# Weight sums stored through GpSimd's queue, the size pass over w2 in halves to another buffer, and spread requests that wait on evacuations, in a two-layer attention and SwiGLU kernel

## Chip, cores and metric

The kernel runs on one core of one Trainium2 chip. The metric is the device time of one execution in microseconds (us), and the number for a kernel is the median of several executions. Profiled executions give in addition a span, which is the time from the first to the last recorded instruction.

## What is computed

The input x is 2048 tokens by 1024 channels in bf16. Two layers, each with the same weights, are applied: attention block A, feed-forward block B, then A and B again, each on a normalised x and with a residual.

```
def A(x):                              # 32 heads of 32 channels
    q, k, v = split(x @ wqkv)          # wqkv: 1024 x 3072
    # each token sees itself and 7 earlier ones, at distances 0, 2, 4, ... 14
    logits = einsum(q, k[idx]) * 32 ** -0.5, masked where idx < 0
    return (softmax(logits) @ v[idx]) @ wo        # wo: 1024 x 1024

def B(x):
    return (silu(x @ w1) * (x @ w3)) @ w2         # w1, w3: 1024 x 3584, w2: 3584 x 1024

x = x + A(layernorm(x)); x = x + B(layernorm(x))
x = x + A(layernorm(x)); x = x + B(layernorm(x))
```

## The kernel before

**Units.** The tokens are cut into four chunks of 512. A unit is one chunk in the B block of one layer, so there are eight units, numbered 0 to 7. The order is skewed: while B works on one chunk, the attention of the next one is computed by VectorE (DVE), and from unit 1 on a q, k, v projection for layer 1 follows a unit. TensorE (PE) does the projections (line 740, `ps`), the output projection of attention (line 688, `po`), w1 (line 1097, `pg`), w3 (line 1106, `pu`), w2 (line 1128, `acc`), and two kinds of small matmuls for attention: `gather` (line 513, tile L) collects the logits of the heads, and `spread` (line 554, tile pe) spreads the softmax weights over the channels again. ScalarE (ACT) does the silus and the copies out of PSUM. PSUM has six banks in the pool `psum`, which all large products share, and two in the pool `side`, for po, L, pe and the sizes.

**Two ways through B.** Units 0 and 1 multiply with the plain weights. Beside that they prepare the weights for the other six units: those use a scheme with seven products of half size in place of eight, on sums and differences of quarters of the weights in fp16. The scaled quarters and their sums are stored to DRAM, in `t_d` for w1 (made in unit 0) and w3 (made in unit 1), and in `t2_d` for w2 (made in unit 1). Units 2 to 7 load them as tiles early, late and t (lines 639 and 630) and multiply in lines 985 and 920.

**How a group is prepared.** The 28 blocks of 128 hidden channels are split as 16 and 12 (`fsplits`), and a group holds four blocks, so each of w1 and w3 has seven groups. `measure` (line 766) sums the squares of a group on ACT. `scales` makes a power of two from it (line 780 on PE, lines 771 to 775 on DVE). `copies` (line 792) writes four scaled quarters with ACT into one of two blocks of the buffer `big`, once for a = 0 and once for a = 1. `differences` (line 804) makes four differences from them with DVE and then stores the block, in lines 806 and 807, as 512 and 384 KB. The next `copies` into the same block must wait until those two transfers have read it. `prepare` places these steps at slots 0 to 7 of a group, which are the places after each pg and each pu. The second differences of a group come in slot 1 of the next one.

**w2.** Unit 0 measures w2: `measure2` (line 831) squares a tile of eight or six blocks of 512 and writes the squares, which nobody reads, into the start of `big`. In unit 1 `transform2` makes the sums: for each f it writes four scaled quarters with ACT (line 848) into block f % 2 of `big`, and its inner function `rest`, called one step later, makes four differences on DVE (line 854) and stores 896 KB in one transfer (line 856). There are eight such steps in the first split and six in the second, one for each group of `acc` products. The q, k, v projection that follows unit 1 evacuates its products into other parts of `big` (line 744), which overlap these blocks.

**Order.** Each engine runs its instructions in the order in which the Python code emits them, apart from POOL (GpSimd), on which no work stands after the start. The code keeps a model of time, `now`, with one clock for PE, DVE, ACT, SP and the DMA, and the functions `pe`, `dve`, `act` and `dma` advance it. `background(until)` emits as much of DVE's queued work (norms, sums, values, scores) as the model expects to fit before a given time; so a changed cost or due time changes the order on all engines from there on. Requests for the small attention matmuls stand in `pe_queue`, first in first out; `pe_requests` emits the head of it once the model's time of PE is 1.5 past the head's due time. `score_steps` appends one request for gather and four for spread in each half chunk; each spread is followed by a copy on ACT (line 556) into At, which frees its bank. All loads and stores go through SP's queue. Weight tiles share six buffers (`wp`), and a load is emitted when a buffer is released. `hsum` is a buffer of sums of activations, which only units 2 to 7 use.

Of the kernel before, what the change touches and what calls it, by code (L numbers as in the profile page):

```python
# [7 lines left out]
FP32 = mybir.dt.float32  # L8
BF16 = mybir.dt.bfloat16
# [3 lines left out]
ACTF = mybir.ActivationFunctionType  # L13
# [4 lines left out]
def kernel(  # L18
# [13 lines left out]
    nc = tc.nc  # L32
    cfg = dict(cfg or {})
    P = 128
# [33 lines left out]
    const = ctx.enter_context(tc.tile_pool(name="const", bufs=1))  # L68
# [28 lines left out]
    def dve(cost, ready=0.0):  # L97
        now["dve"] = max(now["dve"], ready) + cost
        return now["dve"]

    def act(cost, ready=0.0, table=None):
        t = max(now["act"], ready)
        if table is not None and table != now["table"]:
            now["table"] = table
            t += TABLE
        now["act"] = t + cost
        return now["act"] + 0.1
# [91 lines left out]
    size = const.tile([P, 2, NG], FP32, name="size")  # L199
    up_scale = const.tile([P, 2, NG], FP32, name="up_scale")  # L200
    down_scale = const.tile([P, 2, NG], FP32, name="down_scale")
    size2 = const.tile([P, 8], FP32, name="size2")
    total = const.tile([P, 1], FP32, name="total")
    down2 = const.tile([P, 1], FP32, name="down2")
    up2 = const.tile([P, 1], FP32, name="up2")
# [265 lines left out]
        vT = qkvp.tile([P, KT, HALO + TCH], BF16, name="vT")  # L471
        vs[l, h] = vT, load_part(vT, l, 2, h * TCH, True)

    pe_queue = []
    L_at, At_at, Ats, av_done = {}, {}, {}, set()
    halves = [(l, h) for l in range(2) for h in range(NCH * R)]
    BLK = TCH // 4

    def pe_requests(limit=1, must=False):

        while pe_queue and limit and (must or pe_queue[0][0] + 1.5 <= now["pe"]):
            pe_queue.pop(0)[1]()
            limit -= 1

    def score_steps():

        V = nc.vector
        for g, (l, h) in enumerate(halves):
            load_qk(l, h)
            while (l, h) not in qks:  # L490
                yield "blocked"
                load_qk(l, h)
            load_v(l, h)
            qT, kT, ready = qks[l, h]
            psm = wk.tile([P, W, TCH], BF16, name="psm")

            def mul_qk(w_):
                pr = scr.tile([P, KT, TCH], BF16, name="pr", tag="scr")
                k0 = HALO - DIL * w_
                V.tensor_tensor(pr[:], qT[:], kT[:, :, k0:k0 + TCH], op=ALU.mult)  # L500
                return pr

            yield 0.0, ready, lambda: None
            yield from tree(W, mul_qk, lambda w_: psm[:, w_, :])
            load_v(l, h)
            if g + 1 < len(halves):
                load_qk(*halves[g + 1])
            at = {}

            def gather_heads(t):  # L510
                at["L"] = L = side.tile([P, W, BLK], FP32, name="L", tag="sd")
                for a in range(4):
                    nc.tensor.matmul(L[32 * a:32 * (a + 1), :, :], lhsT=gather[:],
                                     rhs=psm[:, :, a * BLK:(a + 1) * BLK], start=True, stop=True)
                at["t"] = pe(3, t) + 0.2

            while g and halves[g - 1] not in At_at:
                yield "blocked"
            t = now["dve"] + 0.2
            pe_queue.append((t, lambda: gather_heads(t)))  # L520
            while "t" not in at:
                yield "blocked"
            L = at["L"]
            mx = smp.tile([P, BLK], FP32, name="mx")
            E = smp.tile([P, W, BLK], BF16, name="E")
            sm_ = smp.tile([P, BLK], FP32, name="sm_")
            rs = smp.tile([P, BLK], FP32, name="rs")
            An = E
            yield 0.0, at["t"], lambda: None
            if h == 0:  # L530
                yield 0.2, 0.0, lambda: V.tensor_tensor(L[0:32, :, 0:HALO], L[0:32, :, 0:HALO], maskT[:],
                                                        op=ALU.add)
            yield 0.68, 0.0, lambda: V.tensor_reduce(mx[:], L[:].rearrange("p w e -> p e w"), op=ALU.max, axis=AX.X)

            def exps():
                V.tensor_tensor(L[:], L[:], mx[:].unsqueeze(1).to_broadcast([P, W, BLK]), op=ALU.subtract)
                nc.scalar.activation(E[:], L[:], ACTF.Exp, scale=scale)  # L537
                at["E"] = act(0.65, now["dve"] + 0.1, "exp")

            yield 0.70, 0.0, exps  # L540
            yield 0.0, at["E"] if "E" in at else 0.0, lambda: None
            yield 0.66, at["E"], lambda: V.tensor_reduce(sm_[:], E[:].rearrange("p w e -> p e w"), op=ALU.add,
                                                         axis=AX.X)
            yield 0.56, 0.0, lambda: V.reciprocal(rs[:], sm_[:])
            yield 0.68, 0.0, lambda: V.tensor_tensor(An[:], E[:], rs[:].unsqueeze(1).to_broadcast([P, W, BLK]),
                                                     op=ALU.mult)
            while g >= 1 and halves[g - 1] not in av_done:
                yield "blocked"
            At = Ats[l, h] = wk.tile([P, W, TCH], BF16, name="At")
            t2 = now["dve"] + 0.2  # L550

            def spread_heads(a, At=At, An=An, t2=t2, key=(l, h)):
                ps = side.tile([P, W, BLK], FP32, name="pe", tag="sd")
                nc.tensor.matmul(ps[:], lhsT=spread[:, a, :], rhs=An[:], start=True, stop=True)
                r = pe(1, t2)
                nc.scalar.copy(At[:, :, a * BLK:(a + 1) * BLK], ps[:])  # L556
                done = act(0.6, r)
                if a == 3:
                    At_at[key] = done

            for a in range(4):
                pe_queue.append((t2, lambda a=a, f=spread_heads: f(a)))

    def value_steps():

# [211 lines left out]
    def scales(m, g):  # L777

        ps = side.tile([P, 1], FP32, name="size", tag="sd")
        nc.tensor.matmul(ps[:], lhsT=ones[:], rhs=size[:, m, g:g + 1], start=True, stop=True)  # L780
        r = pe(1)
        up, down = up_scale[:, m, g:g + 1], down_scale[:, m, g:g + 1]
        background(r)
        scale_of(ps[:], up, down)
        dve(0.8, r)

    def copies(m, g, w, a):

        b = blocks[a]
        KQ = KT // 2  # L790
        for i, (kh, fh) in ((0, (0, 0)), (1, (0, 1)), (3, (1, 0)), (5, (1, 1))):
            nc.scalar.activation(b[:, i], w[:, kh * KQ:(kh + 1) * KQ, fh * 256 + a * P:fh * 256 + (a + 1) * P],  # L792
                                 ACTF.Copy, scale=up_scale[:, m, g:g + 1])
        copied.append(act(2.9, now["dve"] + 0.1))

    copied = []

    def differences(m, g, a):

        b = blocks[a]  # L800
        r = copied.pop(0)
        background(r)
        for out, x, y in ((4, 5, 1), (1, 1, 0), (2, 5, 1), (6, 3, 2)):
            nc.vector.tensor_tensor(b[:, out], b[:, x], b[:, y], op=ALU.subtract)  # L804
        dve(1.85, r)
        nc.sync.dma_start(t_d[m][g][:, 4 * a:4 * (a + 1)], b[:, 0:4])
        nc.sync.dma_start(t_d[m][g][:, 8 + 3 * a:8 + 3 * (a + 1)], b[:, 4:7])
        dma(512, now["dve"])
        dma(384, now["dve"])

    def prepare(u, g, slot, w1t, w3t, junk):

# [14 lines left out]

    def measure2(i, w, n):

        junk = big[:, 0:n * 512].bitcast(BF16).rearrange("p (k c) -> p k c", k=n)  # L830
        nc.scalar.activation(junk, w[:, 0:n, :], ACTF.Square, accum_out=size2[:, i:i + 1])
        act(n * 0.45 + 0.2)

    def scales2():

        ps = side.tile([P, 8], FP32, name="size", tag="sd")
        nc.tensor.matmul(ps[:], lhsT=ones[:], rhs=size2[:], start=True, stop=True)
        r = pe(1)
        background(r)
        nc.vector.tensor_reduce(total[:], ps[:], op=ALU.add, axis=AX.X)  # L840
        scale_of(total[:], up2[:], down2[:])
        dve(1.1, r)

    def transform2(i, f, ws, loaded):

        b = big[:, f % 2 * 4096:f % 2 * 4096 + 3584].rearrange("p (b c) -> p b c", b=7)
        for j, (fh, hh) in ((0, (0, 0)), (2, (0, 1)), (1, (1, 0)), (5, (1, 1))):
            nc.scalar.activation(b[:, j], ws[hh][fh][:, f, :], ACTF.Copy, scale=up2[:])
        r = act(2.5, loaded)

        def rest():
            background(r)
            for out, x, y in ((4, 5, 2), (2, 2, 0), (3, 5, 2), (6, 1, 3)):
                nc.vector.tensor_tensor(b[:, out], b[:, x], b[:, y], op=ALU.subtract)
            dve(1.85, r)
            nc.sync.dma_start(t2_d[i][:, :, f, :], b)
            dma(1000, now["dve"])

        return rest

# [367 lines left out]
```

## Time and profile before

| | |
|---|---|
| median of 8 executions | 1609.94 us (1607.64 to 1612.57) |
| profiled execution: its time | 1612.3 us |
| profiled execution: its span | 1610.6 us |
| PE busy | 1547.3 us, 96% |
| DVE busy | 1332.2 us, 83% |
| ACT busy | 750.1 us, 47% |
| POOL busy | 3.4 us |
| DMA | 423.80 MB, mean 263 GB/s |
| stores t_d<-big on SP | 28 of 512 KB, 28 of 384 KB, 14 of 896 KB; 3.6, 4.4 and 4.5 us to landing (median) |

The span is 1.7 us shorter than the time of the same execution. In the trace, the stages lie so: the first attention projections until 197 us, unit 0 from 197 to 380 us, unit 1 to 566 us, then units 2 to 7. In the rows, "t_d<-big" also names the stores to `t2_d`. A wait is named by who waits, then `<-`, then what it waited for. In a timeline the bracket at the end of a row is the idle time of that engine just before it, and what ended it. A clock of 1.00 is TensorE's full speed.

### The profile page before, as it was taken

The page shows a single profiled execution, that of the slowest core. Times are in us where ns is not written, and L with a number is a line of the kernel's source. Part 1 is how long each engine was busy: PE and PEld are TensorE (multiplying, and loading weights), DVE is VectorE, ACT ScalarE, POOL GpSimd, SP SyncE. Part 2 cuts the span into 40 slices and gives each one's busy share as a digit, 9 for nine tenths or more (in the row PEclk, how much of TensorE's full clock was granted, in tenths as well). Part 3 has the DMA queues.
Part 4 walks back from the last instruction along what each step waited for, and adds up shares of the span by engine and source line. Part 5 has one row for each costly group of instructions (what it writes and reads, how often), then busy time and mean ns, then how long its engine had stood idle before and what let it go on. Part 6 is the DMA issues. An engine that isn't in the chain of part 4 may idle for free.

```text
span 1610.6 us, 24733 instructions
## 1 busy us (share of the span) xinstructions
PE 1547.3 (96%) x9621; PEld 998.3 (62%) x9666; DVE 1332.2 (83%) x2366; ACT 750.1 (47%) x1144; POOL 3.4 (0%) x16
## 2 busy tenths in 40 slices
PE   9999997998977969999999999999999999999999
PEld 7566643443433437866676756858568577676866
DVE  6799795888948958999899999899989999886555
ACT  4333466467747544443346334625345343443423
POOL 0000000000000000000000000000000000000000
PEclk9999998999998999999999999999999999999999
DMA  9544658384896888797969797797978788877885
GB/s 322 162 158 113 197 169 297 118 283 152 268 308 212 294 267 325 244 343 277 284 238 334 289 305 254 277 330 268 300 277 292 263 302 337 298 262 268 335 289 212
DMA packets 262261, 423.80 MB, mean 263 GB/s; under 512 B 72704, under 2 KB 205312, under 8 KB 245888
## 3 DMA queue, kind: packets, MB, share of 16 engines
q1 hardware_dynamic: 262000, 422.10, 77.8%
q8 instruction: 75, 1.23, 0.3%
q14 instruction: 42, 0.34, 0.1%
q10 hardware_dynamic: 144, 0.13, 0.0%
HBM read 338.56 MB, written 67.90 MB: 252 GB/s over the span
## 4 chain that ended last, share of the span: by engine, by line
PE 77%; DMA 9%; DVE 8%; ACT 4%; issue 1%; SPq 1%; ACTq 0%; DVEq 0%
PE st L985 31%; PE ps L740 16%; PE w L920 14%; PE po L688 6%; DMA t_d<-big 5%; PE pg L1097 3%; PE pu L1106 3%; PE acc L1128 2%; DVE pr L500 1%; DVE st L226 1%; DMA x_sb<-in_A_x_dram 1%; DVE big L804 1%; DVE pr L425 1%; ACT big L792 1%; DMA w2t<-in_B_w_dram 1%
## 5 line engine op out<-in xcount | busy, mean ns | idle before, releaser
L740 PE MATMUL ps<-xnT,wqkv 128*128 128x512 f16 (+1 forms) x1469 | 327.6, 383 | 10.8 <-DVE x_sb L1142 9.7
L985 PEld LDWEIGHTS <-early 128*128 128x128 f16 x2688 | 262.7, 98 | 40.4 <-issue 4.4
L740 PEld LDWEIGHTS <-wqkv 128*128 128x128 bf16 x1472 | 211.2, 144 | 123.3 <-issue 17.8
L920 PE MATMUL w<-t,hT 128*128 128x512 f16 x1008 | 226.6, 379 | 0.7 <-DVE hT L891 0.3
L985 PEld LDWEIGHTS <-late 128*128 128x128 f16 x2016 | 197.1, 98 | 29.4 <-issue 0.7
L744 ACT CAST big<-ps 128x512 bf16<-128x512 f32 x184 | 107.0, 587 | 219.5 <-PE ps L740 194.8
L985 PE MATMUL st<-big,early 128*128 128x256 f16 x1344 | 172.2, 273 | 2.9 <-DVE big L282 1.6
L985 PE MATMUL st<-xnT,late 128*128 128x256 f16 x1344 | 174.2, 273 | 0.0
L920 PEld LDWEIGHTS <-hT 128*128 128x128 f16 x1008 | 98.1, 98 | 115.7 <-issue 3.3
L500 DVE TENSOR_TENSOR pr<-qT,kT 128x2048 bf16<-128x2048 bf16 x128 | 155.6, 1215 | 13.7 <-DMA kT<-qkv_d 9.8
L985 PE MATMUL st<-xnT,early 128*128 128x256 f16 x1344 | 164.7, 273 | 0.1
L583 DVE TENSOR_TENSOR tm<-At,vT 128x2048 bf16<-128x2048 bf16 x128 | 155.6, 1216 | 9.7 <-ACT At L556 9.7
L425 DVE TENSOR_TENSOR pr<-pr 128x1024 bf16<-128x1024 bf16 (+1 forms) x256 | 137.1, 549 | 0.5
L425 DVE TENSOR_TENSOR tm<-tm 128x1024 bf16<-128x1024 bf16 (+1 forms) x256 | 136.5, 549 | 0.4
L1011 ACT COPY st<-st 128x512 f32<-128x512 f32 x84 | 48.3, 575 | 148.8 <-PE st L985 145.8
L1128 PE MATMUL acc<-w2t,hT 128*128 128x512 bf16 x436 | 105.3, 397 | 9.8 <-DMA w2t<-in_B_w_dram 8.6
L688 PE MATMUL po<-wo,oT 128*128 128x512 bf16 x489 | 111.4, 379 | 3.2 <-ACT E L537 1.7
L999 DVE SCALAR_TENSOR_TENSOR hT<-st,down_scale,sg 128x512 f16<-128x512 f32 x126 | 93.7, 743 | 16.9 <-PE st L985 16.6
L1097 PE MATMUL pg<-xnT,w1t 128*128 128x512 f16 x448 | 107.5, 383 | 0.0
L1106 PE MATMUL pu<-xnT,w3t 128*128 128x512 f16 x448 | 106.2, 380 | 0.6 <-DMA w3t<-in_B_w_dram 0.6
L994 ACT ACTIVATE sg<-st,down_scale 128x512 bf16<-128x512 f32 x126 | 86.9, 689 | 37.8 <-PE st L985 36.4
L1128 PEld LDWEIGHTS <-hT 128*128 128x128 bf16 x448 | 45.1, 101 | 68.4 <-issue 19.1
(150 smaller groups left out, 1676.5 us busy)
## 6 DMA issues: line engine op xcount, KB each, us to landing
early<-t_d SPq DMA_DIRECT2D x84, 1024.0 KB, 6.3
late<-t_d SPq DMA_DIRECT2D x84, 768.0 KB, 6.4
t<-t_d SPq DMA_DIRECT2D x42, 1024.0 KB, 7.4
t<-t_d SPq DMA_DIRECT2D x42, 768.0 KB, 5.3
wqkv<-in_A_wqkv_dram SPq DMA_DIRECT2D x28, 1024.0 KB, 7.9
qkv_d<-big SPq DMA_DIRECT2D x92, 256.0 KB, 2.7
w1t<-in_B_w_dram SPq DMA_DIRECT2D x14, 1024.0 KB, 6.8
w3t<-in_B_w_dram SPq DMA_DIRECT2D x14, 1024.0 KB, 9.2
```

Source lines behind the costliest of these rows:

```text
L425: nc.vector.tensor_tensor(b[:, 0:m, :], b[:, 0:m, :], b[:, m:2 * m, :], op=ALU.add)
L500: V.tensor_tensor(pr[:], qT[:], kT[:, :, k0:k0 + TCH], op=ALU.mult)
L583: V.tensor_tensor(tm[:], At[:], win, op=ALU.mult)
L688: nc.tensor.matmul(ps[:], lhsT=oT[:, t, j * P:(j + 1) * P], rhs=wo[:, t, hh * 512:(hh + 1) * 512], start=(t == 0), stop=(t == KT - 1))
L740: nc.tensor.matmul(ps[:], lhsT=ws[kk // KH][:, kk % KH, t::KT], rhs=xnT[:, kk, :], start=(kk == 0), stop=(kk == KT - 1))
L744: nc.scalar.copy(sgt[:, t - t0, :], ps[:])
L920: nc.tensor.matmul(out[:], lhsT=lhs[:, k, j * P:(j + 1) * P], rhs=w[:, k, :], start=start and k == 0, stop=k == nq - 1, skip_group_check=True)
L985: nc.tensor.matmul(out[:, a, :], lhsT=w[:, a, blk, k, :], rhs=rhs[:, k, :], start=start and a == 0 and k == 0, stop=k == KQ - 1, skip_grou ...
L999: nc.vector.scalar_tensor_tensor(h16[:, f:f + 2, t0:t0 + HT], src, inv, gates[g, q][:], op0=ALU.mult, op1=ALU.mult)
L1097: nc.tensor.matmul(pg[:], lhsT=w1t[:, kk, fi * P:(fi + 1) * P], rhs=xnT[:, kk, :], start=(kk == 0), stop=(kk == KT - 1))
L1106: nc.tensor.matmul(pu[:], lhsT=w3t[:, kk, fi * P:(fi + 1) * P], rhs=xnT[:, kk, :], start=(kk == 0), stop=(kk == KT - 1))
L1128: nc.tensor.matmul(acc[:], lhsT=hT[:, f, j * P:(j + 1) * P], rhs=tiles[hh][f // nq][:, f % nq, :], start=(f == 0), stop=(f == f1 - f0 - 1))
```

## The change

- The stores of `differences` and of `transform2` are issued by GpSimd (`nc.gpsimd.dma_start`) instead of SP. The model no longer charges SP and the DMA for them, but keeps for each block a time `stored`, 7.0 after DVE's last difference, and the next copies into that block are due no earlier.
- `measure2` squares each tile in two halves and writes into `hsum`; `size2` has 16 columns instead of 8.
- A request in `pe_queue` holds a function for its due time. The first two spreads of a half are due as before. The last two are due 1.0 before the end of the evacuation that stands two places before them in the model, and the model's cost of such an evacuation is 0.5 instead of 0.6.
- `copies` are due 0.1 after the scale they use (`up_at`) instead of 0.1 after the whole of DVE's time.

```
     def pe_requests(limit=1, must=False):
-        while pe_queue and limit and (must or pe_queue[0][0] + 1.5 <= now["pe"]):
+        while pe_queue and limit and (must or pe_queue[0][0]() + 1.5 <= now["pe"]):
...
-            pe_queue.append((t, lambda: gather_heads(t)))
+            pe_queue.append((lambda: t, lambda: gather_heads(t)))
...
                 nc.scalar.copy(At[:, :, a * BLK:(a + 1) * BLK], ps[:])
-                done = act(0.6, r)
+                done = act(0.5, r)
+                spread_at.append(done)
...
             for a in range(4):
-                pe_queue.append((t2, lambda a=a, f=spread_heads: f(a)))
+                pe_queue.append(((lambda t2=t2: t2) if a < 2 else (lambda: spread_at[-2] - 1.0), lambda a=a, f=spread_heads: f(a)))
...
         scale_of(ps[:], up, down)
-        dve(0.8, r)
+        up_at[0] = dve(0.8, r) + 0.1
...
-        copied.append(act(2.9, now["dve"] + 0.1))
+        copied.append(act(2.9, max(up_at[0], stored[a])))
...
         dve(1.85, r)
-        nc.sync.dma_start(t_d[m][g][:, 4 * a:4 * (a + 1)], b[:, 0:4])
-        nc.sync.dma_start(t_d[m][g][:, 8 + 3 * a:8 + 3 * (a + 1)], b[:, 4:7])
-        dma(512, now["dve"])
-        dma(384, now["dve"])
+        nc.gpsimd.dma_start(t_d[m][g][:, 4 * a:4 * (a + 1)], b[:, 0:4])
+        nc.gpsimd.dma_start(t_d[m][g][:, 8 + 3 * a:8 + 3 * (a + 1)], b[:, 4:7])
+        stored[a] = now["dve"] + 7.0
...
     def measure2(i, w, n):
-        junk = big[:, 0:n * 512].bitcast(BF16).rearrange("p (k c) -> p k c", k=n)
-        nc.scalar.activation(junk, w[:, 0:n, :], ACTF.Square, accum_out=size2[:, i:i + 1])
-        act(n * 0.45 + 0.2)
+        k = n // 2
+        junk = hsum[:].bitcast(BF16).rearrange("p k t -> p (k t)")[:, 0:k * 512].rearrange("p (k c) -> p k c", k=k)
+        nc.scalar.activation(junk, w[:, 0:k, :], ACTF.Square, accum_out=size2[:, 2 * i:2 * i + 1])
+        nc.scalar.activation(junk, w[:, k:n, :], ACTF.Square, accum_out=size2[:, 2 * i + 1:2 * i + 2])
+        act(n * 0.45 + 0.4)
...
     def transform2(i, f, ws, loaded):
...
-        r = act(2.5, loaded)
+        r = act(2.5, max(loaded, stored[f % 2]))
...
             dve(1.85, r)
-            nc.sync.dma_start(t2_d[i][:, :, f, :], b)
-            dma(1000, now["dve"])
+            nc.gpsimd.dma_start(t2_d[i][:, :, f, :], b)
+            stored[f % 2] = now["dve"] + 7.0
```

More of the change, by code (lines that the diff above doesn't have):

```diff
@@ L201 @@
     down_scale = const.tile([P, 2, NG], FP32, name="down_scale")
-    size2 = const.tile([P, 8], FP32, name="size2")
+    size2 = const.tile([P, 16], FP32, name="size2")
     total = const.tile([P, 1], FP32, name="total")
@@ L472, in load_v @@
         vs[l, h] = vT, load_part(vT, l, 2, h * TCH, True)
-    pe_queue = []
+    pe_queue, spread_at = [], []
     L_at, At_at, Ats, av_done = {}, {}, {}, set()
@@ L793, in copies @@
                                  ACTF.Copy, scale=up_scale[:, m, g:g + 1])
-        copied.append(act(2.9, now["dve"] + 0.1))
-    copied = []
+        copied.append(act(2.9, max(up_at[0], stored[a])))
+    copied, stored, up_at = [], [0.0, 0.0], [0.0]
     def differences(m, g, a):
@@ L828, in measure2 @@
     def measure2(i, w, n):
-        junk = big[:, 0:n * 512].bitcast(BF16).rearrange("p (k c) -> p k c", k=n)
-        nc.scalar.activation(junk, w[:, 0:n, :], ACTF.Square, accum_out=size2[:, i:i + 1])
-        act(n * 0.45 + 0.2)
+        k = n // 2
[3 more added lines that the diff above has]
+        act(n * 0.45 + 0.4)
     def scales2():
-        ps = side.tile([P, 8], FP32, name="size", tag="sd")
+        ps = side.tile([P, 16], FP32, name="size", tag="sd")
         nc.tensor.matmul(ps[:], lhsT=ones[:], rhs=size2[:], start=True, stop=True)
```

## The prediction, on record before the changed kernel ran

> **What bounds the kernel now.** I read the waits of TensorE first, then busy time by stretches of 40 us, then PE's timeline at each hole, and last ACT's and SP's timelines there. PE is busy for 1547.3 of 1610.6 us, so all that PE ever stands idle is 63.3 us. Its waits (total, times, longest):
>
> ```profile
> PE pe L554 <- ACT At L556: 26.1, 4, 16.0
> PE ps L740 <- DVE x_sb L1142: 9.7, 4, 4.8
> PE acc L1128 <- DMA w2t<-in_B_w_dram: 8.6, 5, 4.2
> ```
>
> Three waits make 44.4 us, and all are in units 0 and 1, where the weights are prepared. The stretches (length, PE, PEld, DVE, ACT, POOL busy, clock, DMA share, GB/s):
>
> ```profile
> 240.00:280.00 40.00, 30.08 (x138) 13.08 (x138) 24.28 (x55) 27.41 (x37) 0.00 (x0) 0.92 0.90 293
> 360.00:400.00 40.00, 35.73 (x155) 15.74 (x156) 33.55 (x60) 29.31 (x31) 0.00 (x0) 0.91 0.47 154
> 440.00:480.00 40.00, 33.25 (x146) 14.55 (x147) 22.54 (x53) 17.59 (x27) 0.00 (x0) 0.96 0.93 309
> 480.00:520.00 40.00, 26.37 (x112) 11.56 (x112) 29.28 (x59) 29.24 (x40) 0.00 (x0) 0.79 0.65 210
> 560.00:600.00 40.00, 27.68 (x113) 14.66 (x113) 22.98 (x54) 15.81 (x28) 0.00 (x0) 0.91 0.80 259
> 640.00:680.00 40.00, 39.86 (x330) 32.28 (x330) 36.78 (x68) 18.90 (x31) 0.00 (x0) 1.00 0.79 262
> ```
>
> PE lacks 9.9, 4.3, 6.8, 13.6 and 12.3 us here: 46.9 of the 63.3. From 640 us on it is full. The holes on PE's timeline (start, length, instruction, idle before it):
>
> ```profile
> 278.24 1.07 PE L554 MATMUL pe<-E,spread 128*128 128x512 bf16 x2 [8.52 <-ACT At L556]
> ...
> 367.28 6.56 PE L1128 MATMUL acc<-w2t,hT 128*128 128x512 bf16 x18 [4.17 <-DMA w2t<-in_B_w_dram]
> ...
> 493.63 1.07 PE L554 MATMUL pe<-E,spread 128*128 128x512 bf16 x2 [15.97 <-ACT At L556]
> ```
>
> PE does not lack work there: a spread stands in its order before ready work, needs a bank of the two in `side`, and the copy that frees the bank stands on ACT behind other things. What those are:
>
> ```profile
> 270.87 2.56 ACT L792 ACTIVATE big<-w1t,up_scale 128x512 f16<-128x512 bf16 x4 [6.20 <-DMA t_d<-big]
> 274.01 3.62 ACT L831 ACTIVATE big<-w2t 128x4096 bf16<-128x4096 bf16 x1 [0.58 <-DMA t_d<-big]
> ...
> 481.60 5.17 ACT L848 ACTIVATE big<-w2t,up 128x512 f16<-128x512 bf16 x8 [3.95 <-DMA t_d<-big]
> ...
> 589.65 3.52 ACT L744 CAST big<-ps 128x512 bf16<-128x512 f32 x7 [7.40 <-DMA t_d<-big]
> ```
>
> ACT waits for stores out of `big`. And why those are late, on SP:
>
> ```profile
> 447.65 3.38 SPq L806 DMA_DIRECT2D t_d<-big  x1
> ...
> 455.89 0.39 SPq L643 DMA_DIRECT2D w2t<-in_B_w_dram  x1
> ...
> 465.98 29.55 SPq L856 DMA_DIRECT2D t_d<-big  x7
> ```
>
> The queue is in order. A store waits for DVE's differences and holds the weight loads behind it (SP waited 135.4 us at L806 for DVE, the longest time 28.5), and a store behind two loads of 1 MB takes 8.64 us (at 241.04) or 10.40 (345.17), where the shortest L806 landing took 2.6. **The bound of these stages is a ring: store, ACT's copies, DVE's differences, store**, with SP's order making it longer.
>
> **What the skill says.** "DMA: Bandwidth & Descriptors", Queues, rings and completion order: each DMA engine goes round the queues with work, packet by packet. A store in its own queue then no longer waits for the whole load before it; it shares. No row before shows two loaded queues: q1 has all but 1.7 of 423.8 MB. "SBUF — State Buffer", Who interferes with whom: GpSimd cannot write its DMA descriptors while DVE runs in a two-port mode; tensor_tensor has none, which for descriptors is called inferred. In units 0 and 1 nearly all of DVE's work is tensor_tensor; untested here, POOL issued no transfer. "TensorE: Matmul & The Clock Gate", Part 1: after an idle window of about 3.4 us the clock is halved for about as long. The trace agrees: the eight pg matmuls at 494.70 took 3.41 us, later ones 1.73. That is 1.7 us lost on one group, and the group after it lost 0.35 more (2.08 against 1.73), so I add 2 us to every long hole.
>
> **The change, part by part.** Prices: for one half of a group's sums (0.92 MB; two transfers, or one of 896 pieces for w2) let L be the time from DVE's last difference to the landing. Below: 4.5, the median L856 landing, with SP nearly alone. The same page prices a GpSimd transfer (Anatomy of one DMA) at 2.0 us + bytes/436e3, an estimate of 4.1, so the price itself isn't higher. Sharing half of the 350 GB/s that the saturated stretches show gives 0.92/175 = 5.2 us + 2.0 = 7.2. Above: 10.4, the worst before. I take L = 6.5. Waiting on POOL holds up nothing: in its order the 70 stores are all that is left.
>
> (a) *Hole at 265 to 278* (9.3 us idle, 0.6 more at 245, 2 cold). L831 now writes to `hsum`, idle until unit 2, so its wait is gone; the halves cost eight more starts and eight more accumulator reads of 0.19, some 0.4 us each, 3 us in all beside an ACT that has 12 of 40 us free. The last two spreads are asked for after an evacuation, so PE takes acc matmuls first. SP's fourth w2t, issued at 275.71, needs only ACT's copies of w1t (L792), now about 267; landing at 273 it precedes its use (261.8 + 4 x 3.45 + 1.7 = 277). Saved: 12.
>
> (b) *Hole at 363* (4.2 + 2). L792's second set waited 10.40 us to 355.57; with L = 6.5 it starts near 352, ends at 354.5, and the fourth w2t leaves then instead of at 360.4. The 6.8 us it took give 361.3, before 363.1. The DMA engines are saturated here (345 to 360 us: 344 to 360 GB/s), so I count 5 of 6.2.
>
> (c) *Holes at 440 to 494* (20.4 + 4). The second set of L792 waited until 450.64; now its store starts at 438 and lands by 445. Differences, scale and the next store free the first w2 block at about 453. Then eight steps with two blocks: two steps take 2.56 (ACT) + 1.85 (DVE) + 0.2 + L, that is 11.1, where before they took 8.95 (472.64 to 481.60) with loads held back. Copies end at 453 + 3 x 11.1 + 5.1 = 491.4, 5 us before the old 496.5. PE gains more than that: no spread stands in its way. Its eight groups end at 472, the new order has two output tiles (6.9 us) among them, and five free banks give 5 x 1.73 = 8.6 us of the next group: work to 487.5. Stall left: 4 to 5 us with its cold clock. Saved: 19. Each us of L is 4 us here (start and three pairs).
>
> (d) *Holes at 566 to 600* (12.3 + 2). L744's first copy still waits for the last store, as both use `big`. Fourth w2t no longer behind L806: first step near 550.5, last copies 550.5 + 2 x 11.1 + 5.1 = 577.8, differences 580, landing 586.5 against 589.6. Saved: 3. Again 4 us for each us of L.
>
> (e) *Afterwards.* From the built order, with the durations of the rows above, about 10 us less score and value work stands on DVE before unit 2 begins. It must be done between 640 and 1440 us, where DVE is busy 37 of 40; the slack of 3 in each 40 us, 60 in all, covers it. If not, `po` waits for it. A delayed spread also holds the next request behind it in its queue and the values that read At. I charge 5.
>
> Sum: 12 + 5 + 19 + 3 - 5 = 34. On the profiled execution, 1610.6 becomes 1576.6, with 1.7 us outside the span 1578.3; that execution lies 2.4 above the median, so the median is about **1576**.
>
> **Rivals.** *R1, slower: stores by GpSimd are slow.* If descriptors come slowly or DVE starves them, (c) and (d) lose 8 us for each us of L; 34 us are gone at L = 6.5 + 34/8 = 10.8. That is above the worst landing before, and it must be the usual one; at L = 13 the time is 1610 + 8 x 2.2 = 1628. For: 896 pieces, never tried here. Against: the transfer's price of 4.1. *R2, given back: DVE.* All the deferred work returns as waits of PE in units 2 to 5, and the delayed spreads cost the values 5 us more: 15 instead of the 5 charged in (e), 1576 + 10 = 1586. For: DVE at 92%. Against: the rows name 7.0 us of PE waits in all of the 970 us after 640. *R3, the DMA engines are the bound.* From 440 to 470, in steps of 5 us, they carried 341 to 374 GB/s already; loads that start earlier only delay the stores, L stays near 8.5, (c) and (d) lose 16: 1592. *R4, nothing moves*: other waits replace these and the time stays within 3 us of 1610.
>
> **How the numbers follow.** Forecast 0.47 (own range 1562 to 1584); R2 0.17; R3 0.17; R4 0.05; R1 0.14. Faster by over 0.2% (about what a measurement can tell from no change): 0.47 + 0.17 + 0.17 = 0.81; same 0.05; slower 0.14. The range takes in L from 4.5 (16 less) and R3 with some of (e) on top: 1558 to 1606, leaving out R1 and most of R4.
>
> **What would show it.** Right: PE's wait pe L554 <- At falls from 26.1 to under 5; SP no longer waits 135 us for L804; the w2 steps run 10 to 12 us for two; a hole of some us is left before 500 and one before 590; the clock row loses its dents. Wrong: stores landing 10 us and more after DVE's differences (R1), DVE rows before `po` or new PE waits past 640 (R2), ACT waiting as long for t_d with DMA share at 1 (R3).

## The result and the profile after

The changed kernel takes **1601.3 us** (median of 10, 1599.81 to 1603.41) beside 1610.05 of the kernel before on the same chip: a ratio of 0.9945, 95% interval 0.9937 to 0.9953. That is 8.8 us faster, where 34 were forecast, inside the range given. The direction was right and the size wrong by a factor of four. The profiled execution took 1601.1 us. Line numbers after are higher by one or two (L554 is the same, L740 is now L741, L856 is L858). The page's head, then its clock row, of the changed kernel:

```profile
span 1599.4 us, 24803 instructions
PE 1543.8 (97%) x9622; PEld 998.2 (62%) x9666; DVE 1332.3 (83%) x2366; ACT 750.6 (47%) x1161; POOL 46.0 (3%) x86
...
PEclk9999999999999799999999999999999999998999
```

TensorE's waits (total, times, longest) are no longer those of before:

```profile
PE st L987 <- DVE big L282: 12.4, 1, 12.4
PE ps L741 <- DVE x_sb L1144: 10.1, 4, 4.2
PE po L689 <- DVE x_sb L694: 7.6, 1, 7.6
PE ps L741 <- ACT big L745: 4.6, 1, 4.6
```

The wait `pe L554 <- At`, 26.1 us before, is gone, as forecast. Two large waits are new: 12.4 us in one place, and 7.6 for an output tile. By stretches (length, PE, PEld, DVE, ACT, POOL busy, clock, DMA share, GB/s):

```profile
240.00:280.00 40.00, 39.84 (x188) 18.09 (x190) 28.00 (x57) 31.13 (x40) 4.27 (x8) 1.00 1.04 364
440.00:480.00 40.00, 34.36 (x154) 15.21 (x156) 29.80 (x61) 26.60 (x38) 5.34 (x6) 0.91 0.78 261
480.00:520.00 40.00, 37.41 (x176) 17.08 (x177) 33.25 (x73) 25.46 (x36) 6.43 (x12) 1.00 0.81 287
520.00:560.00 40.00, 25.24 (x90) 11.48 (x88) 35.11 (x73) 16.10 (x27) 5.38 (x6) 0.79 0.78 265
1440.00:1480.00 40.00, 27.61 (x173) 18.07 (x172) 17.42 (x30) 8.28 (x14) 0.00 (x0) 0.83 0.59 199
```

PE now fills 240 to 280 (30.08 before), and 480 to 520 gains 11 us. But 520 to 560 has 25.24 (39.84 before), and 1440 to 1480, where nothing was touched, falls to 27.61 from 38.26. In the clock row the two dents of before, in slices 7 and 13, are gone; slices 14 and 37 have new ones.

Stretches at fixed times compare different work. So I count, in PE's timeline of each kernel, the large matmuls done so far, each at its full-clock duration, and ask when a kernel reaches the same amount. The **lead** over the kernel before, in us, one profiled execution each; time is that of the kernel before:

```
at (before's us)      283   372   456   500   520   594  1471  1493   end
after                14.9  22.4  22.1  36.6  35.0  22.6  24.9  11.5  11.5
q_only                1.6   7.6   1.4   5.5   5.3   1.1   0.0  -0.6  -1.1
g_only                6.9   5.3   4.3  20.9   6.6   8.9   9.3  -4.1  -4.8
after_sp             13.2  13.0   2.8  17.9  16.6   8.1  10.9  -2.2  -2.8
qmg                  13.3  17.9  17.6  32.9  13.9  13.6  16.5   3.1   3.2
last_sp              14.3  21.5  20.3  34.9  33.4  26.3  29.1  16.4  15.9
slk12_last_sp        14.3  21.5  21.1  34.8  34.1  24.5  24.4  26.0  25.8
no_o                 13.7  21.6  20.7  24.5  23.0   9.9  11.8  -1.8  -2.9
no_o_later           14.4  22.3  21.4  33.5  25.7  17.3   5.3  -6.3  -7.2
```

The first row tells the story. At 500 us the lead is 36.6 us, about the forecast of the first three gains, 36. Then 10.6 are lost from 520 to 618, where the lead is 24.4, and 13.4 at one place after 1471.

Some 2 us of every row are not the change's. *after* has a lead of 2.5 by 230 us, and *m_only* (below), which has nothing new up to there, one of 1.8. In the trace of before, 40 matmuls of L740 that begin at 64.14 took 10.54 us; in those two traces they took 8.85. So the profiled execution of before was slow by about that much from the start.

**The first loss, about 10.6 us.** ACT's timeline at the end of unit 1, then GpSimd's, then SP's:

```profile
516.66 2.56 ACT L850 ACTIVATE big<-w2t,up 128x512 f16<-128x512 bf16 x4 [8.26 <-DMA t_d<-big]
...
542.54 2.56 ACT L850 ACTIVATE big<-w2t,up 128x512 f16<-128x512 bf16 x4 [3.09 <-DMA t_d<-big]
558.34 3.03 ACT L745 CAST big<-ps 128x512 bf16<-128x512 f32 x6 [13.23 <-DMA t_d<-big]
```
```profile
548.41 0.89 POOL L858 DMA_DIRECT2D t_d<-big  x1 [3.70 <-issue]
```
```profile
505.37 1.01 SPq L644 DMA_DIRECT2D w2t<-in_B_w_dram  x1
506.47 2.32 SPq L626 DMA_DIRECT2D wqkv<-in_A_wqkv_dram  x2
...
543.29 2.69 SPq L626 DMA_DIRECT2D wqkv<-in_A_wqkv_dram  x4
```

The last store is issued at 548.41 and releases ACT at 558.34: 9.9 us. From 543.29 on SP issues 4 MB of wqkv loads. In the kernel before these stood behind the store in SP's queue:

```profile
577.46 7.21 SPq L856 DMA_DIRECT2D t_d<-big  x2
584.76 4.07 SPq L625 DMA_DIRECT2D wqkv<-in_A_wqkv_dram  x4
```

There ACT's copy began at 589.65, after a wait of 7.40. Taking a store out of an ordered queue also takes away its precedence over what followed it. Added up, from the first `acc` product of this stage to L745: 54.8 us after (503.58 to 558.34), 47.8 before (541.87 to 589.65). Of the 7.0, the last wait makes 5.8. And before, 3.6 us of an output tile lay inside that time (L688 at 544.46); after, it comes later. 7.0 + 3.6 = 10.6.

The same happened at the start of this stage. The first step (L850 at 516.66) waited 8.26 us for a store of w3 sums, issued at 508.45 and 508.98, which took 8.1 and 8.8 us to land: the fourth w2t and two wqkv loads had been issued from 505.37 on. Before, these three stood behind the stores of w3 (549.26 and 550.08, after 548.84), which landed in 2.6 to 3.7 us. This part is read from the traces; no run tried it.

**The second loss, 13.4 us.** PE's timeline at the change from unit 6 to unit 7 in the changed kernel, then DVE's and SP's:

```profile
1437.58 6.85 PE L689 MATMUL po<-wo,oT 128*128 128x512 bf16 x31
1444.27 7.93 PE L922 MATMUL w<-t,hT 128*128 128x512 f16 x36
1452.04 1.04 PE L987 MATMUL st<-xnT,early 128*128 128x256 f16 x8
1465.47 3.57 PE L987 MATMUL st<-big,early 128*128 128x256 f16 x16 [12.39 <-DVE big L282]
```
```profile
1453.28 0.99 DVE L254 TENSOR_SCALAR xn<-x_sb,mv,rstd 128x1024 f16<-128x1024 bf16 x2
1464.72 0.69 DVE L282 TENSOR_TENSOR big<-xnT 128x1024 f16<-128x1024 f16 x1 [10.46 <-DMA xnT<-xn]
```
```profile
1455.27 7.36 SPq L257 DMA_TRANSPOSE xnT<-xn  x2
```

And the same place in the kernel before:

```profile
1443.37 3.40 PE L688 MATMUL po<-wo,oT 128*128 128x512 bf16 x15
...
1452.94 3.40 PE L688 MATMUL po<-wo,oT 128*128 128x512 bf16 x15
...
1466.78 10.53 PE L920 MATMUL w<-t,hT 128*128 128x512 f16 x48
1479.77 1.91 PE L985 MATMUL st<-big,early 128*128 128x256 f16 x16 [1.58 <-DVE big L282]
```

Before, the last chunk's output tiles stood 34 and 24 us ahead of the end of unit 6's products (1477.3), and the norm, its transposes and the sums that follow were hidden. After, both come in one block 14.6 us ahead of that end (1452.2); the norm is written when PE has run out, and the transposes land 10.5 us later. It is the last unit: no other work is left to put in between.

### The profile page after: what moved, and what is told of

Same layout as the page of the kernel before. It is cut to its first block, busy times and chain, and to the rows that moved or that the text cites. A ratio compares the mean times of both kernels' runs of the same rounds, so it can differ in the third digit from the quotient of the medians.

```text
span 1599.4 us, 24803 instructions
## 1 busy us (share of the span) xinstructions
PE 1543.8 (97%) x9622; PEld 998.2 (62%) x9666; DVE 1332.3 (83%) x2366; ACT 750.6 (47%) x1161; POOL 46.0 (3%) x86
## 4 chain that ended last, share of the span: by engine, by line
PE 56%; DVE 5%; ACT 1%; DMA 1%; SPq 0%; issue 0%; DVEq 0%; ACTq 0%
PE st L987 29%; PE w L922 15%; PE ps L741 7%; PE po L689 5%; DVE st L226 1%; DMA xnT<-xn 1%; DVE hT L1001 1%; DVE tm L584 0%; DVE tm L425 0%; PE pe L554 0%; DVE pr L500 0%; DVE x_sb L907 0%; DVE xn L254 0%; SPq L257 0%; DVE pr L425 0%
## 5 line engine op out<-in xcount | busy, mean ns | idle before, releaser
L741 PE MATMUL ps<-xnT,wqkv 128*128 128x512 f16 (+1 forms) x1469 | 331.1, 385 | 15.0 <-DVE x_sb L1144 10.1
L741 PEld LDWEIGHTS <-wqkv 128*128 128x128 bf16 x1472 | 211.5, 144 | 130.1 <-issue 26.0
L745 ACT CAST big<-ps 128x512 bf16<-128x512 f32 x184 | 107.0, 585 | 237.9 <-PE ps L741 197.2
L987 PE MATMUL st<-big,early 128*128 128x256 f16 x1344 | 174.2, 274 | 15.8 <-DVE big L282 12.4
L500 DVE TENSOR_TENSOR pr<-qT,kT 128x2048 bf16<-128x2048 bf16 x128 | 155.6, 1216 | 14.0 <-DMA kT<-qkv_d 10.7
L584 DVE TENSOR_TENSOR tm<-At,vT 128x2048 bf16<-128x2048 bf16 x128 | 155.6, 1215 | 11.2 <-ACT At L556 11.2
L1130 PE MATMUL acc<-w2t,hT 128*128 128x512 bf16 x437 | 98.1, 379 | 1.4 <-DVE hT L1112 0.9
L689 PEld LDWEIGHTS <-oT 128*128 128x128 bf16 x512 | 50.4, 99 | 67.5 <-issue 11.0
```

The source lines that it names most:

```text
L584: V.tensor_tensor(tm[:], At[:], win, op=ALU.mult)
L689: nc.tensor.matmul(ps[:], lhsT=oT[:, t, j * P:(j + 1) * P], rhs=wo[:, t, hh * 512:(hh + 1) * 512], start=(t == 0), stop=(t == KT - 1))
L741: nc.tensor.matmul(ps[:], lhsT=ws[kk // KH][:, kk % KH, t::KT], rhs=xnT[:, kk, :], start=(kk == 0), stop=(kk == KT - 1))
L745: nc.scalar.copy(sgt[:, t - t0, :], ps[:])
L987: nc.tensor.matmul(out[:, a, :], lhsT=w[:, a, blk, k, :], rhs=rhs[:, k, :], start=start and a == 0 and k == 0, stop=k == KQ - 1, skip_grou ...
L1130: nc.tensor.matmul(acc[:], lhsT=hT[:, f, j * P:(j + 1) * P], rhs=tiles[hh][f // nq][:, f % nq, :], start=(f == 0), stop=(f == f1 - f0 - 1))
```

## The experiments

Each ratio below is to the kernel before in the same session; its median moved from 1608.7 to 1610.1 between sessions, so a difference of two times from different sessions is uncertain by about 1 us.

**One part at a time.** The theory at this point: the stores' queue is what brings the gain, and the order that comes from the gate on spreads brings the late hole.

*q_only*: the kernel before with its three stores issued by GpSimd; the model still charges SP.

```
-        nc.sync.dma_start(t_d[...], ...)
+        nc.gpsimd.dma_start(t_d[...], ...)
```

> The kernel before with only the 70 stores of weight sums moved to GpSimd's queue; its model of time still charges SP and the DMA for them, so the order of PE, DVE and ACT is that of before. Theory (the order took the gain back): the holes at 265, 363, 440 and 460 shrink because stores and loads no longer stand in each other's way, the 12 us hole ahead of unit 7 does not appear because DVE's order is the old one; 15 to 25 us faster than before, 1585 to 1595. Rival (GpSimd's queue itself costs, or its traffic slows the late transposes): no better than 1601, with a hole ahead of unit 7.

Measured 1614.55 us, ratio 1.0036 (1.0024 to 1.0049): slower, a miss, and without the rival's late hole (2.1 us, before 1.6). The stores no longer hold loads back, and yet the spreads wait as long as before, since in the order they still stand ahead of ready work:

```profile
PE pe L554 <- ACT At L556: 28.5, 4, 17.0
```

*after_sp*: the changed kernel with its three stores on SP again.

```
-        nc.gpsimd.dma_start(...)
+        nc.sync.dma_start(...)
```

> The changed kernel with its stores given back to SP: the order of PE, DVE and ACT is that of the changed kernel, SP carries stores and loads again. Theory (the order took the gain back): the hole of about 12 us ahead of unit 7 stays, since it comes from the order, and the early holes come back in part, as loads stand behind stores: 1605 to 1625. Rival (the queue took it back): the hole ahead of unit 7 is gone.

Measured 1615.89, 1.004 (1.0025 to 1.0055). The new order on SP's queue costs 7 us; the late hole is there (12.26 us).

*m_only*: the size pass over w2 alone.

```
+        junk = hsum[:].bitcast(BF16)...[:, 0:k * 512]...
+        nc.scalar.activation(junk, w[:, 0:k, :], ACTF.Square, accum_out=size2[:, 2 * i:2 * i + 1])
+        nc.scalar.activation(junk, w[:, k:n, :], ACTF.Square, accum_out=size2[:, 2 * i + 1:2 * i + 2])
```

> The kernel before with only the size pass over w2 in halves into the activation-sum buffer. Its wait for the stores was 4.6 us, of which 0.6 lay in the 8.5 us hole at 278. Theory: 0 to 5 us faster, 1605 to 1610, as the copies of the spreads still stand behind ACT's copies that wait for a store. Rival (the size pass was what held the spread): 9 to 12 us faster, the hole at 278 gone.

Measured 1607.21, 0.9991 (0.9983 to 0.9999). Part (a) needs the gate as well: a hole of 8.26 us stays at 276.

*g_only*: the gate on spreads alone, with the evacuation's cost of 0.5.

```
-                pe_queue.append((t2, lambda a=a, f=spread_heads: f(a)))
+                pe_queue.append(((lambda t2=t2: t2) if a < 2 else (lambda: spread_at[-2] - 1.0), ...))
```

> The kernel before with only the spread requests waiting on evacuations (and the model's 0.5 in place of 0.6). Theory: waits of spreads for At fall from 26 us to under 5, but the holes at 363 and 460 (loads behind stores) stay and silus and DVE's adds still wait behind the stores: 5 to 15 us faster, 1595 to 1605. Rival (spreads only name the hole, something else ends at the same time): 0 to 3 us, the same holes under another name.

Measured 1618.33, 1.0054 (1.0039 to 1.0069): slower, a miss. The spreads still wait 10.4 us, and the w2 loads, which stand behind stores, cost 10.5 (8.6 before). The lead reaches 20.9 at 500 and falls to 6.6 at 520, where PE waits 3.1 us for an addition (L1143), 5.1 for a spread's bank and 3.0 for a size's bank. The late hole is there too (12.55). It is in after, after_sp, g_only and qmg, which have the gate's order, and in neither q_only nor m_only. So the queue of the stores doesn't make it; the order does.

*qmg*: all of the change but the times `stored` and `up_at`; the model charges the stores to its DMA clock, as before.

```
-        copied.append(act(2.9, max(up_at[0], stored[a])))
+        copied.append(act(2.9, now["dve"] + 0.1))
-        r = act(2.5, max(loaded, stored[f % 2]))
+        r = act(2.5, loaded)
-            stored[f % 2] = now["dve"] + 7.0
+            dma(1000, now["dve"])
```

> The changed kernel without what its model knows of the stores and of the scale: stores on GpSimd, size pass in halves and gated spreads, but the model still charges SP and the DMA and lets ACT copy at once. Theory (three edits must act together for the early gain, the model's time of 7.0 adds little): by 480 us of before it is 20 us or more ahead, loses about as much at the last store and 12 us ahead of unit 7: 1600 to 1607. Rival (the gain comes from the plan that knows when blocks come free): ahead by less than 12 there, 1610 or more.

Measured 1608.12, 0.999 (0.9983 to 0.9997), just above the range expected. Up to 500 us it leads by 32.9; at 520 by 13.9. Between 468 and 490 us of its own time PE waits 4.5 us for an addition, 4.2 for a spread's bank and 2.5 for a size's bank. The copies that free these two banks stand on ACT behind L851, which waits for stores out of `big`; that the missing times made this order is argued, not tried one by one. Against the 1601.3 of the whole, the two times together are worth some 7 us. So the parts give their gain only together: the queue alone costs 6 us, the gate alone 10, and both with the size pass give 1.5.

**The last store.** *last_sp*: the changed kernel with the last store of unit 1 on SP, ahead of the wqkv loads.

```
-            nc.gpsimd.dma_start(t2_d[i][:, :, f, :], b)
+            (nc.sync if (i, f) == (1, 5) else nc.gpsimd).dma_start(t2_d[i][:, :, f, :], b)
```

> The changed kernel with only the last of the 70 stores (second split, sixth step) on SP, ahead of the four loads of wqkv; order of all else unchanged. In the changed kernel this store took 10.2 us beside these loads and the first copy of the projection waited 13.2 us. Theory (the store is slow because it shares the DMA engines with 4 MB of loads that SP's order held back before): it lands in 5 to 6 us and the time falls by 4 to 5, to 1596 to 1598. Rival (PE waits there for DVE's adds and would wait as long): 0 to 1 us.

Measured 1596.35, 0.9919 (0.9904 to 0.9934), 5.0 us below the changed kernel (4.2 by the ratios), as the theory had it. ACT's timeline:

```profile
543.79 2.56 ACT L850 ACTIVATE big<-w2t,up 128x512 f16<-128x512 bf16 x4 [3.08 <-DMA t_d<-big]
554.88 3.52 ACT L745 CAST big<-ps 128x512 bf16<-128x512 f32 x7 [8.54 <-DMA t_d<-big]
```

The wait is 8.54 in place of 13.23; the 4.7 are what the store lost when the loads ran beside it.

**The late hole.** *after06*: the model's cost of an evacuation back to 0.6.

```
-                done = act(0.5, r)
+                done = act(0.6, r)
```

> The changed kernel with one number of its model put back: an evacuation of a spread costs 0.6 again instead of 0.5. In its built order the output tiles of the last chunk stand in unit 6 where they stood before the change, in two blocks, not in one late block. Theory (the 12 us hole ahead of unit 7 comes from the order that the model makes, by chance of where the last values end): the hole shrinks to under 3 us and the early gain stays, 1586 to 1592. Rival (any order made with the gate leaves DVE too late): the hole stays, 1598 to 1604.

Measured 1599.36, 0.9937 (0.9924 to 0.9949). The late hole went (2.09), so it hangs on the order. But the new order has other holes in unit 1, a lead of 18.8 at 520; the gain of 9 to 15 us did not come. A cost in this model is no knob for one place. *after06_last_sp* has both edits.

> Both edits at once. If the two losses are independent, their gains add up: 1581 to 1588. If the second only fills a wait that the first leaves, no better than after06 alone by more than 1 us.

Measured 1596.06, 0.9915 (0.9900 to 0.9929), a miss for the same reason.

*out_pool*: the output stores on GpSimd, so that they don't stand ahead of the transposes on SP.

```
-                nc.sync.dma_start(xout[:, n, hh * 512:(hh + 1) * 512], xs)
+                nc.gpsimd.dma_start(xout[:, n, hh * 512:(hh + 1) * 512], xs)
```

> The changed kernel with the output stores issued by GpSimd instead of SP, so that at the change from unit 6 to unit 7 SP's queue holds no output stores ahead of the two transposes. Theory (DVE hands over the normalised rows too late): the transposes start at most 1 to 2 us earlier and the 12 us hole stays above 10, 1598 to 1601. Rival (SP's queue delays the transposes): the hole falls to about 6 or less, 1594 or less.

Measured 1600.88, 0.995 (0.9936 to 0.9963), in the expected range. The late hole falls from 12.39 to 9.99: SP's queue is 2.4 of it, the lateness of the norm the rest. The time stays that of the changed kernel.

*slk12*: the allowance with which units 2 to 7 let DVE's queued work start, 0.8 to 1.2 in the six calls of `background` in their products. The order up to unit 1 stays.

```
-            background(r + 0.8)
+            background(r + 1.2)
```

> The changed kernel with one edit that acts from unit 2 on: before each of DVE's evacuations the plan fills DVE up to 1.2 past the product's end instead of 0.8. Units 0 and 1 keep the changed kernel's order; from unit 2 on values and scores come earlier, and the last chunk's output tiles stand in unit 6 about as early as before the change. Theory (the 12 us hole ahead of unit 7 is score and value work that units 0 and 1 leave undone and the plan never catches up): the hole shrinks to under 3 us and all else stays, 1586 to 1591. Rival (DVE has no room from 640 us on, earlier values only make PE wait for evacuations): as much is lost in units 2 to 6, 1598 to 1603.

Measured 1588.92, 0.9873 (0.9857 to 0.9889), in the expected range: 12.4 us below the changed kernel (11.6 by the ratios), by six numbers that touch neither queues nor instructions' cost. Its lead is 22.5 us at 1471 and 24.2 at 1493, so the late hole is gone. *slk12_last_sp* adds the last store on SP.

> The edit of 1.2 and the last store on SP together. If the two losses are independent: 1581 to 1587. If not: no better than the better one alone.

Measured **1585.97**, 0.9852 (0.9838 to 0.9867), the best version. PE's timeline at the change of unit, then DVE's:

```profile
1422.79 3.40 PE L689 MATMUL po<-wo,oT 128*128 128x512 bf16 x15
...
1442.76 10.53 PE L922 MATMUL w<-t,hT 128*128 128x512 f16 x48
1453.13 1.04 PE L987 MATMUL st<-xnT,early 128*128 128x256 f16 x8
1454.00 1.91 PE L987 MATMUL st<-big,early 128*128 128x256 f16 x16
```
```profile
1434.70 0.54 DVE L254 TENSOR_SCALAR xn<-x_sb,mv,rstd 128x1024 f16<-128x1024 bf16 x1
1440.48 0.69 DVE L282 TENSOR_TENSOR big<-xnT 128x1024 f16<-128x1024 f16 x1
```

The output tile is back between the products, the norm is written 18 us ahead of the products' end, and no hole is left. *slk14_last_sp*: 1.4.

> As the last one, with 1.4 in place of 1.2; the last output tiles stand earlier still. Theory: the hole is gone already at 1.2, so the time is within 3 us of it, and worse if DVE's evacuations now hold PE's banks. Rival (some of the hole was left at 1.2): 2 to 5 us faster.

Measured 1592.37, 0.9893 (0.9878 to 0.9907), 6.4 us worse and outside the 3 us expected: too early is bad as well. Small waits of `st` from 658 on take the lead from 27.7 to 19.1 by 1471.

**What is missing in (c).** The hole of 7.6 us at 444 belongs to an output tile that stands ahead of ready `acc` products. *no_o*: no output tiles among the first eight w2 steps of unit 1 (the third argument says whether `between` may emit them).

```
-                    between(hold and not lastsplit, lastsplit and hh == 0 and j == 1 and not hold)
+                    between(hold and not lastsplit, lastsplit and hh == 0 and j == 1 and not hold,
+                            (u, split) != (1, 0))
```

> The changed kernel, with no output tiles of attention put among the first eight w2 steps of unit 1; they follow in the second split. Theory: the hole of 7.6 us at 444 is an output tile that stands in PE's order ahead of ready work and waits for a bank in `side` whose reader (L694) stands on DVE behind the differences of the weights. Without it PE goes on with its own groups there: that hole is gone, the lead on the kernel before at 456 us grows from 22 to 26 us or more, and (c) comes near its 19. The late hole stays (the order of unit 6 isn't touched), so the time is 1594 to 1598. Rival: PE has no other work there (the weights aren't ready), and the hole comes back under another name, w2t or At; then the lead at 500 stays at 36 or falls, and the time is 1600 or more.

Measured 1614.19, 1.0027 (1.0018 to 1.0037): a miss. The hole at 444 is gone, but the tile came right after, and a gather behind it waited for its bank:

```profile
469.04 0.62 PE L513 MATMUL L<-psm,gather 128*32 128x512 bf16 x4 [16.66 <-DVE x_sb L694]
```

*no_o12ls* is the best version with the same edit.

> The same with the background's slack of 1.2 and the last store on SP, to be read against that version without it (1585.97). Theory: 4 to 6 us faster than that, 1580 to 1582. Rival: 1586 or more.

Measured 1597.17, 0.9927 (0.9910 to 0.9943), a miss: 11 us worse than without it. *no_o_later* adds to *no_o* that the tiles stay away until the differences are over.

```
-                        between(hold)
+                        between(hold, tiles=u != 1 or f0 == 0 or f >= f0 + 5)
```

> As the run before without output tiles among the first eight w2 steps of unit 1, and none ahead of the sixth w1 product of the second split either: there they stood behind the last differences (DVE at 468) and a gather behind them waited 16.7 us for the bank. Theory: PE has ready work after the w2 products, and only the place of the output tiles took it away: from 445 to 470 PE shows no hole above 2 us, and the lead on the kernel before at 500 us is 40 us or more. Rival: PE runs out of ready work there whatever the order (weights, or banks whose evacuations stand behind the differences): a hole of 5 us or more for another reason, and a lead at 500 of 37 or less. The time of the whole is not what is asked, since the order of the later units shifts with it; 1590 to 1615.

Measured 1621.08, 1.0076 (1.0054 to 1.0098), and the rival holds. With no tile in its way PE stops in its own products, shown by its timeline and then by DVE's:

```profile
448.31 1.89 PE L1099 MATMUL pg<-xnT,w1t 128*128 128x512 f16 x8
456.31 3.57 PE L1108 MATMUL pu<-xnT,w3t 128*128 128x512 f16 x8 [6.11 <-DVE x_sb L1144]
```
```profile
446.76 0.68 DVE L1144 TENSOR_TENSOR x_sb<-x_sb,acc 128x512 bf16<-128x512 bf16 x1
...
453.86 1.80 DVE L856 TENSOR_TENSOR big<-big 128x512 f16<-128x512 f16 x4 [4.95 <-ACT big L850]
455.58 0.68 DVE L1144 TENSOR_TENSOR x_sb<-x_sb,acc 128x512 bf16<-128x512 bf16 x1
```

PE's `acc` groups hold the six banks, and each is freed by an addition (L1144) that stands on DVE behind differences (L856) of the ring. PE gets three groups of the next split in, then waits 6.11 and 3.46 us for additions and 2.56 for a size pass (L767) on ACT. The lead at 500 is 33.5, not above the changed kernel's 36.6. The place of the output tile didn't cost the missing time; the ring did.

## Why the prediction was right in direction and wrong in size

The yardstick is the lead, with the two losses in it: 2.5 us by 230, then 12.4 + 7.5 - 0.3 + 12.9 - 10.6 + 0.5 - 13.4 makes the 11.5 at the end. The spans differ by 11.2; of the medians 8.8 is left, since the profiled execution before was 2.4 above its median. Beside the forecast of 34, (c) fell short by 6.1, (d) by 13.6 and (e) by 8.4; these three are the steps that failed.

- **(a), 12 forecast, 12.4 measured** (2.5 to 14.9). Right in mechanism and size. m_only shows that the moved size pass alone doesn't do it.
- **(b), 5 forecast, 7.5 measured.** Right in kind. The first part's stage ends a little after 283: the first pg after it starts at 302.07 before and at 286.03 after, a lead of 16.0. So 1.1 of the 7.5 belongs to (a), and (b) gained about 6.4, its whole hole of 6.2. (The 10.40 us named there are the store's landing; ACT itself stood idle for 3.17 of them.)
- **(c), 19 forecast, 12.9 measured.** The ring's pace was about right: two steps take 10.5 us (DVE's L856 at 430.14 and, three pairs on, at 461.58) where 11.1 were reckoned. The term that failed is "five free banks give 5 x 1.73": PE gets three groups (*no_o_later*), as the banks are freed by additions behind L856. And of the two output tiles counted as cover (6.9 us), the second was itself what waited. The stall left is 7.6 + 1.2 + two of 0.2, and 1.5 of lower clock after it (15 matmuls of the output tile took 4.7 us, where 15 took 3.2 at 212.01): about 11 us, not 4 to 5.
- **(d), 3 forecast, 10.6 lost.** The step that failed is the landing of a store, L = 6.5, at both ends of the stage. Counted from the stage's first `acc` product, the forecast had the first step at 8.6 us (550.5) and L744 at 44.6 (586.5); measured are 13.1 and 54.8. Of these 10.2 the first step is 4.5: it waited for the stores of w3, which shared with loads that had stood behind them. The last landing is 3.9: from DVE's last difference it took 10.4 us in place of 6.5, beside the four wqkv loads. The pace between makes the rest, 1.8. The working let one load behind a store go earlier (the fourth w2t) and overlooked that it, and the six wqkv loads, then run beside the stores that ACT waits for. *last_sp* moved only the last store and gave 4 to 5 us back; the first step and the output tile of 3.6 us, which lay elsewhere, are read from the traces and not tried.
- **(e), 5 charged, 13.4 lost.** "The slack of 3 in each 40, 60 in all, covers it" failed, though not as R2 had it: PE's lead stays between 22 and 26 us from 618 to 1471, so on balance the deferred work cost PE nothing there, and DVE's sum is the same (1332.2 and 1332.3). Slack on an engine is of use only if the order puts the work into it. The values of the last chunk ended late, and the price was paid once, at the last unit. *slk12*, and the kernels with and without the hole, show this.

Of the rivals, *R1* is out: the w2 stores land in 4.9 us (median), and the steps keep their pace. *R3* names the right resource for the stores at both ends of (d) only. *R4* is out: the spreads' waits are gone. *R2* had the right size (15) at the wrong place. With (a) to (c) as they came and (d) and (e) as forecast, the sum would have been 2.5 + 12.4 + 7.5 + 12.9 + 3 - 5, 33 us. That this is near the forecast's 34 is in part luck: the 2.5 belongs to the trace of before, and (b) came out over its forecast while (c) came out under.

## What to carry to other kernels

Before a transfer leaves an ordered queue, list what stands behind it there: that work is let go too, and it competes with the transfer if somebody waits for the landing. Where a planner decides the order, a moved due time is not paid for where it is made but where the last cover ends, so look at the last unit, and try the planner's allowance before the kernel's work. And count free banks by who frees them: a bank behind a stalled engine isn't free.

## What the runs showed of the hardware

The landings of the changed kernel (KB each, median us from issue):

```profile
t_d<-big POOLq DMA_DIRECT2D x28, 512.0 KB, 6.7
t_d<-big POOLq DMA_DIRECT2D x14, 896.0 KB, 4.9
t_d<-big POOLq DMA_DIRECT2D x28, 384.0 KB, 7.3
```

From SP the same stores took 3.6, 4.5 and 4.4. By the medians, stores from GpSimd are thus 2.9 to 3.1 us slower for w1 and w3 and 0.4 for w2. Single ones differ by what runs beside them: a 512 KB store took 2.9 us where the DMA engines carried 246 GB/s meanwhile (305.67) and 9.5 where they carried 388 (510.30). Beside 4 MB of loads the last one of 896 KB held ACT for 9.9 us from its issue; on SP ahead of these loads, for 5.7. That agrees with the Trainium skill, "DMA: Bandwidth & Descriptors", Queues, rings and completion order: queues with work take turns. Issuing took GpSimd 0.54 us for nearly every transfer of 384 or 512 KB (the first took 0.71) and 0.89 to 0.91 for one of 896 pieces. "SBUF — State Buffer", Who interferes with whom, infers that tensor_tensor doesn't hold up GpSimd's descriptors; the trace agrees: an issue of 512 KB took 0.54 us at 252.07, where DVE ran nothing, and at 235.25, wholly beside a tensor_tensor. Nor was DVE held up: its products of q and k (L500) took 1216 ns, before 1215.
